# Another written order for the steps of a retention and GELU feed-forward kernel

## The chip, the cores and the metric

The kernel runs on one core of one Trainium2 chip. The metric is device time in microseconds (us): the median of three runs of the kernel before is 294.59 (294.44 to 296.1).

## What is computed

Two stages follow one another: retention (linear attention with a decay by distance) over 8 batches, 8 heads, 576 positions and 64 values per head, and a feed-forward layer with a tanh-GELU over the 4608 resulting rows.

```
q, k, v: (8, 8, 576, 64)     w_in: (512, 2048)     w_out: (2048, 512)

scores = q @ k.T / 8
gamma  = 1 - 2 ** (-5 - head)
ret    = scores * where(i >= j, gamma ** (i - j), 0)      # i: row of q, j: row of k
attn   = ret @ v
x      = attn with the heads side by side                 # (8 * 576, 512)
h      = x @ w_in
g      = 0.5 * h * (1 + tanh(sqrt(2 / pi) * (h + 0.044715 * h ** 3)))
out    = g @ w_out                                        # (4608, 512)
```

## The kernel before

**Units.** Each batch of 576 rows is cut into five units: four of 128 rows and a tail of 64, so unit u is part u % 5 of batch u // 5, and there are 40. The products of decay powers with q and v stand for the decay matrix; between the parts of a batch a state (sum of k times v) is carried in f32 and cast to f16 for the products. Units 0, 2, 5 and 7 are "wide": each of them stands for two units that are handled together (0 and 1, 2 and 3, and so on). The feed-forward layer goes in nine blocks t of 512 rows and sixteen groups fc of 128 hidden columns. From block 5 on the first product, and for most row pairs the second one, is a Strassen-Winograd product: seven block products instead of eight, with sums of blocks before (SBUF, VectorE) and after (out of PSUM).

**The order is written out by hand.** The string ORDER (line 17) is a list of 1369 steps; a loop at the end of the kernel calls one small function for each. The five engines and their queues run asynchronously, but each one takes its own instructions in the order in which the steps stand, so the string sets what stands behind what on TensorE (PE), VectorE (DVE), ScalarE (ACT), GpSimd (POOL) and SyncE (SP, which issues the loads, stores and DMA transposes). The steps that the change and the prediction speak of:

- `L,u,n` loads page n of unit u (0 is q, 1 is k, 2 is v) from SP (lines 206 to 241). A page is a slot of a pool of 21, nine once the feed-forward sums need the room; a load takes the slot that has been free longest, and its program waits for the cast that last read it. The program also lets every SP copy wait for the one eight before it.
- `I,g` and `J,g` load an eighth of w_in and of w_out, with a cast to f16, from GpSimd's queue (line 255). I,6 and I,7 serve columns 1536 to 2047 (fc 12 to 15), I,2 and I,3 fc 4 to 7, I,0 and I,1 fc 0 to 3, I,4 and I,5 fc 8 to 11; each pair is two halves of the sum over 512.
- `b`, `c`, `g` make the decay tables, the masks with the row powers gend, and the row powers gseg; `Z,i` zeroes a buffer of the f16 state; `w` loads ScalarE's table of the GELU.
- `q,u`, `k,u`, `v,u` scale or cast a page to f16 (lines 441 and 457, line 286 for a plain cast), `t` transposes it on PE (line 514) and `y` copies that out; `D,u` is the DMA transpose of later units (line 504). A last letter says by which engine: v VectorE (the default of q), g GpSimd, a ScalarE.
- `X` (line 640) and `Y` (line 657) are state products and scores of a wide unit, `m` the product with the mask out of PSUM (lines 665 and 722), `R` the attention product of a wide unit (lines 686 and 698), `B,u,w` the scores of unit u and the attention product of unit w, `a`, `o` and `z` the state's sum, decay and cast (lines 746, 754, 764 and 286), and `x` the copy of the result to xT in f16 (lines 607 to 620). There is one PSUM buffer for scores, two banks of pool h and two of pool o.
- `N,t,fc,half` is the first feed-forward product for two fc and half of the 512 rows, `M,t,fc` for one fc and all rows, `M,t,fc,part` for four fc and a quarter of the rows (all at line 790); `F` and `G` are their GELU out of PSUM (line 798).
- `O,t,u` is a quarter of a plain second product (line 816). `H`, `T` are sums for the second Winograd product, `W` (line 904) its block products, `V` its sums and copies out; `U`, `s` are sums for the first one, `A` (line 1001) its products, `l` its sums and copies and `f` its GELU (line 1019). `S` is a store. The sums are at line 850, where all Winograd sums have one helper: they are told apart by tile, tsum and ssum (T, H), pages and hc (U, s, l), ost (V).
- `K,n` is n products of the identity with itself, whose result nobody reads (line 1046).

The loop that calls them:

```
    for step_ in steps:
        name, *args = step_.split(",")
        do[name](*[int(a) if a.lstrip("-").isdigit() else a for a in args])
```

Of the kernel before, what the change touches and what calls it, by code (L numbers as in the profile page):

```python
# [24 lines left out]
N,0,0,1 G,0,9 J,2,g M,0,8 L,7,2 t,5,k,o z,3,1,v F,0,0,1 N,0,12,1 q,7,g G,0,8 y,5,k,a J,3,g N,0,14,1  # L25
Y,5,0 J,4,g k,7,g X,5 F,0,12,1 F,0,14,1 M,0,10 m,5,0 N,0,2,1 a,5,1,g J,7,g t,7,q,o L,9,0 a,6,1
G,0,10 B,-1,4 z,5,1,v Y,5,1 J,5,g m,5,1 M,0,11 F,0,2,1 N,0,6,1 t,7,k,o x,4 J,6,g y,7,k,v y,7,q,a R,5
O,0,4 O,0,0 o,6,1 F,0,6,1 Y,7,0 x,5 x,6 G,0,11 N,1,4,0 N,1,0,0 F,1,4,0 F,1,0,0 O,0,1 O,0,5 L,14,1
L,9,1 N,1,14,0 F,1,14,0 v,7,g H,0,1,5,v m,7,0 U,1,0 N,1,2,0 F,1,2,0 Y,7,1 X,7 L,9,2 a,7,1 z,7,1,a
N,1,10,0 O,0,6 N,1,6,0 F,1,6,0 m,7,1 q,9,g k,9,g a,8,1 z,6,1,v O,0,7 U,2,0 L,11,0 T,1,0,v e,0,1,v  # L30
H,0,1,2,v T,1,1,v R,7 v,9,g L,13,0 j,2,g F,1,10,0 D,9 T,2,1,v x,7 N,1,12,0 x,8 q,11 L,10,0 H,0,1,4,v
W,0,1,1 O,0,2 L,14,2 F,1,12,0 q,10,g L,10,1 N,1,12,1 L,11,1 F,1,12,1 T,2,0,v O,0,3 T,3,1,v B,9,-1
e,0,0,a T,4,0,v k,10,v V,0,1,0,v L,10,2 L,14,0 D,10 N,1,8,0 q,13 N,1,0,1 L,12,0 W,0,1,5 F,1,8,0
F,1,0,1 N,1,2,1 T,4,1,v N,1,14,1 F,1,2,1 L,11,2 k,11,g F,1,14,1 D,11 L,13,1 W,0,1,6 m,9 i,2,g
V,0,1,1,a N,1,8,1 T,3,0,v v,10,v j,4,g L,16,0 N,1,10,1 F,1,8,1 W,0,1,7 z,8,1,v B,10,9 V,0,1,3,a
L,12,1 x,9 m,10 V,0,1,4 N,1,4,1 W,0,1,4 F,1,10,1 a,10,0,g N,1,6,1 a,10,1 z,10,1,a W,0,1,3 v,11,g
z,10,0,v H,1,0,5,v B,11,10 V,0,1,5,v L,12,2 q,12 m,11 F,1,6,1 W,0,1,2 q,14 k,13,g a,11,0 F,1,4,1
W,1,0,1 x,10 N,2,10,0 L,15,0 V,1,0,0,a k,12,g N,2,14,0 H,1,0,2,v F,2,10,0 F,2,14,0 H,1,1,5,v V,0,1,6
V,0,1,2 v,12,v W,1,0,6 H,1,1,2,v L,16,1 j,3,v D,12 N,2,8,0 L,15,2 N,2,4,0 V,1,0,1,v L,13,2 D,13
L,15,1 a,11,1 o,11,1 z,11,0,a W,1,1,1 F,2,8,0 W,1,0,7 F,2,4,0 v,14,g B,12,11 V,1,1,0,v H,1,0,4,v  # L40
v,15,v i,5,a S,0,1 q,15,g a,12,0 z,11,1,a v,13,g i,0,a L,19,1 N,2,0,0 U,1,1 m,12 W,1,1,6 x,11 L,18,0
V,1,0,3,a z,12,0,g N,2,6,0 a,12,1 S,0,3 F,2,0,0 N,2,2,0 W,1,0,4 B,13,12 V,1,1,1,v k,15,v W,1,1,7
F,2,6,0 a,13,0 m,13 V,1,1,3,v V,1,0,5,a q,16 k,16,a W,1,0,2 a,13,1 N,2,12,0 k,14,g F,2,2,0 x,12
z,12,1,a N,2,14,1 D,14 F,2,12,0 W,1,0,5 z,13,1,v z,13,0,a W,1,1,4 S,0,0 L,16,2 B,14,13 L,18,2 L,17,1
F,2,14,1 V,1,1,5,a D,15 x,13 N,2,4,1 V,1,0,2,a L,17,0 L,17,2 H,1,1,4,v W,1,1,5 V,1,0,4,v F,2,4,1
N,2,12,1 L,24,0 v,16,g W,1,0,3 V,1,1,4,v F,2,12,1 m,14 N,2,0,1 B,15,14 V,1,0,6,v a,15,0,g k,17,v
S,0,2 m,15 F,2,0,1 N,2,10,1 W,1,1,3 F,2,10,1 H,2,0,5,v D,16 q,17 L,18,1 k,19,a N,2,2,1 L,20,0
# [1071 lines left out]
```

## Time and profile before

| | us |
|---|---|
| median of 3 runs (lowest, highest) | 294.59 (294.44, 296.1) |
| the profiled execution's own time | 295.5 |
| its span | 293.8 |
| TensorE busy | 280.0 |
| VectorE busy | 225.7 |
| ScalarE busy | 166.6 |
| GpSimd busy | 95.7 |

The span is the stretch that the profiler shows; the time of that execution is 1.7 us longer. Matmul rows carry a modelled end, so that neighbours overlap by some tens of ns. A row of a timeline gives start, duration, engine, line, operation, what it writes and reads, how many instructions were merged, and in brackets the idle time before it with what ended it. An engine's wait for several things is put down to the one that came last. Durations of GpSimd are rough. DMA-issuing rows of SP and GpSimd tell how long the issue took, not the transfer.

### The profile page before, as it was taken

What the parts mean: (1) busy time and instruction counts of PE and PEld (TensorE: products, weight loads), DVE (VectorE), ACT (ScalarE), POOL (GpSimd) and SP (SyncE); (2) the same over time, 40 slices, a digit from 0 to 9 for tenths busy, and PEclk for the clock granted to TensorE, in tenths of its full rate; (3) what the DMA queues carried; (4) which work ended last, traced back from release to release, by engine and by line L of the source; (5) the groups of instructions that cost most, each with busy time, mean ns of one, the idle gap of its engine ahead of it and who ended that gap; (6) DMA issues with size and microseconds to landing.
All of it is one profiled execution on the core that took longest, in us unless ns stands there. A gap on an engine that the chain in (4) does not pass through costs nothing.

```text
span 293.8 us, 9639 instructions
## 1 busy us (share of the span) xinstructions
PE 280.0 (95%) x4042; PEld 233.0 (79%) x4042; DVE 225.7 (77%) x446; ACT 166.6 (57%) x325; POOL 95.7 (33%) x157
## 2 busy tenths in 40 slices
PE   7697999999999999999999899999999999999995
PEld 2366767788888888888888778878887788888874
DVE  6684874986976798748758798899988989985841
ACT  2464763456655534656457558578576697655510
POOL 7841791202531321434643534644313301000000
PEclk9999999999999999999999999999999999999999
DMA  6999999949989979999998979997948430110112
GB/s 159 312 247 212 310 203 207 186 94 225 169 207 233 198 168 196 222 206 159 248 206 196 184 163 197 197 188 193 181 87 187 109 126 2 38 74 36 74 71 108
DMA packets 136428, 49.77 MB, mean 169 GB/s; under 512 B 118209, under 2 KB 130881, under 8 KB 136385
## 3 DMA queue, kind: packets, MB, share of 16 engines
q1 hardware_dynamic: 132032, 44.97, 70.6%
q0 software_dynamic: 4352, 4.20, 8.5%
q8 instruction: 31, 0.51, 0.8%
q14 instruction: 13, 0.10, 0.1%
HBM read 36.70 MB, written 9.44 MB: 157 GB/s over the span
## 4 chain that ended last, share of the span: by engine, by line
PE 77%; DVE 11%; DMA 5%; issue 2%; ACT 1%; SPq 1%; POOL 1%; DVEq 0%; POOLq 0%; ACTq 0%
PE bank L904 29%; PE bank L790 21%; PE bank L1001 14%; PE bank L816 4%; DMA w_in_sb<-in_moe_w_in_dram 3%; DVE ssum L850 2%; DVE pages L850 2%; PE sk L574 2%; PE x L550 2%; DMA pages<-in_q_dram 2%; PE sk L584 1%; PE x L595 1%; PE bank L1031 1%; DVE sz L764 1%; DVE hc L850 1%
## 5 line engine op out<-in xcount | busy, mean ns | idle before, releaser
L790 PE MATMUL bank<-xT,w_in_sb 128*128 128x256 f16 (+1 forms) x608 | 79.0, 279 | 1.8 <-ACT xT L607 0.9
L798 ACT ACTIVATE gT<-bank 128x512 f16<-128x512 f32 x80 | 47.0, 597 | 39.5 <-PE bank L790 39.2
L790 PEld LDWEIGHTS <-w_in_sb 128*128 128x128 f16 x608 | 57.5, 98 | 13.2 <-DMA w_in_sb<-in_moe_w_in_dram 2.5
L904 PEld LDWEIGHTS <-ssum 128*128 128x128 f16 x512 | 49.8, 98 | 6.8 <-DVE ssum L850 0.9
L904 PE MATMUL bank<-tsum,ssum 128*128 128x256 f16 x384 | 49.3, 273 | 0.3 <-DVE ssum L850 0.3
L904 PEld LDWEIGHTS <-gT 128*128 128x128 f16 x384 | 37.0, 98 | 4.4
L441 POOL TENSOR_TENSOR v<-pages,dec 128x512 f16<-128x512 f32 (+1 forms) x24 | 24.2, 1010 | 48.5 <-DMA pages<-in_v_dram 26.6
L286 POOL CAST sz<-s 64x256 f16<-64x256 f32 x36 | 17.3, 479 | 62.1 <-DVE s L746 51.6
L904 PE MATMUL bank<-w_out_sb,gT 128*128 128x256 f16 x256 | 32.9, 273 | 0.0
L1001 PEld LDWEIGHTS <-pages 128*128 128x128 f16 x256 | 24.2, 98 | 7.1 <-issue 2.9
L1001 PE MATMUL bank<-pages 128*128 128x256 f16 x192 | 27.9, 273 | 1.9 <-DVE pages L850 1.3
L722 DVE TENSOR_TENSOR ret<-sk,mask 128x512 f16<-128x512 f32 (+1 forms) x32 | 19.8, 618 | 9.8 <-PE sk L584 5.2
L850 DVE TENSOR_TENSOR ost<-u,bank 128x256 f32<-128x256 f32 x48 | 19.4, 416 | 9.5 <-PE bank L904 9.3
L850 DVE TENSOR_TENSOR ssum<-gT,ssum 128x1024 f16<-128x1024 f16 x32 | 24.0, 754 | 0.1
L284 ACT COPY hc<-bank 128x512 f32<-128x512 f32 x27 | 15.8, 586 | 14.1 <-PE bank L1001 13.8
L850 DVE TENSOR_TENSOR ssum<-gT 128x2048 f16<-128x2048 f16 (+1 forms) x20 | 21.3, 1063 | 2.7 <-ACT gT L798 2.1
L850 DVE TENSOR_TENSOR hc<-hc,bank 128x512 f32<-128x512 f32 x29 | 19.8, 684 | 4.0 <-PE bank L1001 3.8
L1001 PEld LDWEIGHTS <-w_in_sb 128*128 128x128 f16 x192 | 18.6, 98 | 2.9 <-DVE pages L850 0.6
L441 POOL TENSOR_TENSOR qk<-pages,dec 128x512 f16<-128x512 f32 (+1 forms) x16 | 17.1, 1070 | 9.7 <-DMA pages<-in_q_dram 4.8
L746 DVE TENSOR_TENSOR s<-s,sk 128x256 f32<-128x256 f32 x36 | 15.0, 416 | 5.8 <-PE sk L584 4.5
L1001 PE MATMUL bank<-xT,w_in_sb 128*128 128x256 f16 x128 | 19.2, 273 | 0.0
L1019 ACT ACTIVATE gT<-hc 128x512 f16<-128x512 f32 x29 | 17.8, 630 | 2.0 <-DVE hc L850 2.0
(117 smaller groups left out, 445.9 us busy)
## 6 DMA issues: line engine op xcount, KB each, us to landing
out_dram<-ost SPq DMA_DIRECT2D x35, 256.0 KB, 2.6
pages<-in_q_dram SPq DMA_DIRECT2D x32, 256.0 KB, 5.1
pages<-in_k_dram SPq DMA_DIRECT2D x24, 256.0 KB, 4.4
pages<-in_v_dram SPq DMA_DIRECT2D x24, 256.0 KB, 4.4
pages<-in_v_dram SPq DMA_DIRECT2D x4, 512.0 KB, 12.5
pages<-in_k_dram SPq DMA_DIRECT2D x4, 512.0 KB, 6.9
w_in_sb<-in_moe_w_in_dram POOLq DMA_DIRECT2D x8, 256.0 KB, 10.2
w_out_sb<-in_moe_w_out_dram POOLq DMA_DIRECT2D x8, 256.0 KB, 7.9
```

What stands on the lines that cost most here:

```text
L284: nc.scalar.copy(out=o, in_=i)
L286: (nc.vector if eng == "v" else nc.gpsimd).tensor_copy(out=o, in_=i)
L441: eng.tensor_tensor(out=out, in0=pages[:, page_of[s["u"], i], 0:n], in1=dec[:, i // 2, s["j"], 0:n].unsqueeze(2).to_broadcast([128, n, D]) ...
L722: nc.vector.tensor_tensor(out=ret[:, :, 0:n], in0=now["two"][:, :, 0, 0:n], in1=mask.unsqueeze(1).unsqueeze(1).to_broadcast([128, 2, n, G] ...
L746: nc.vector.tensor_tensor(out=s32, in0=state[0], in1=kv, op=ALU.add)
L790: nc.tensor.matmul(hps[:, i, :], w_in_sb[:, ct, 128 * (fc + i) : 128 * (fc + i) + 128], xT[:, ct, TB * t % XR + lo : TB * t % XR + hi], st ...
L798: nc.scalar.activation(out=gTs[t][:, fc : fc + TB // (hi - lo), lo:hi], in_=h.pop((t, fc, lo)), func=AF.Gelu_apprx_tanh, bias=0.0, scale=1.0,)
L816: nc.tensor.matmul(ops[t, tcc], gTs[t][:, ft, 128 * tcc : 128 * tcc + 128], w_out_sb[:, ft, :], start=(ft == 0), stop=(ft == NFC - 1),)
L850: (nc.vector if eng == "v" else nc.gpsimd).tensor_tensor(out=out, in0=a, in1=b, op=op)
L904: nc.tensor.matmul(p["ps", bank][:, HN * col : HN * col + HN], a[:, k], b[:, k], start=(k == 0 and fresh), stop=(k == HK - 1), skip_group_ ...
L1001: nc.tensor.matmul(p["ps", bank][:, n], w[:, c, 128 * n : 128 * n + 128], x[:, c], start=(n == 0 and c == 0 and i in (1, 2, 5)), stop=(c = ...
L1019: nc.scalar.activation(out=gTs[t][:, f : f + 2, o : o + 256], in_=p["ps", 0] if i == 0 else p["c", i], func=AF.Gelu_apprx_tanh, bias=0.0, ...
```

## The change

Only ORDER changes, from 1369 to 1371 steps. The steps up to the 279th and those behind the 540th stand in another order; in between (with a few swaps by one place) the two orders are the same. What is computed stays the same.

- Ahead of all stand now `b c g,g`, the tables and masks, and the first load is q of unit 0 (`L,0,0`), whose cast (`q,0,g`) follows at once; before, three other loads, a zeroing and the issue of one piece of w_in stood ahead of it. The load of k of unit 0 (`L,0,1`) moves from third to seventh among the L steps. v of units 0 and 2 is scaled by GpSimd instead of VectorE, q of unit 4 the other way round.
- In block 0 the four steps `M,0,8` to `M,0,11` and the halves `N,0,4` and `N,0,6` become four quarters `M,0,4,0` to `M,0,4,3` and halves `N,0,8` and `N,0,10`. `w` moves behind the first GELUs, so that ScalarE's table load stands ahead of the first of them.
- The first products of block 0 stand behind `Y,2,1`, `t,5,q`, `X,2` and `Y,2,0`; before, they stood ahead of them or among them. There are 35 dummy products for 38.
- Behind the 540th step loads, casts, sums and copies are in a new order and in part on other engines (of the V copies nine go from ScalarE to VectorE and eight the other way; of the state's casts ten leave GpSimd and seven go to it, and so on), and three pairs of ssum differences are split or joined (`H,6,0,5`, `H,7,0,5`, and `H,7,1,1` with `H,7,1,3`).

```diff
 ORDER = """
-Z,0,g L,4,1 L,0,2 L,0,1 Z,1,v g,g Z,3,v c k,0,a L,0,0 b I,6,g L,2,0 v,0,v K,4 K,4 K,4 K,4 t,0,k,h
-y,0,k,v q,0,g Z,5,v X,0 I,7,g K,4 K,1 t,0,q,h I,2,g L,2,1 q,2 y,0,q,v a,0,1,g z,0,1,a I,3,g a,1,1
-K,4,o K,3,o Y,0,1 L,2,2 Z,2,g L,4,0 m,0,1 k,2,a K,4 K,2 Y,0,0 m,0,0 o,1,1 t,2,k,h L,5,0 t,2,q,h
-y,2,k,a R,0 L,5,1 I,1,g y,2,q,v x,1 x,0 L,4,2 I,0,g z,1,1,g K,4 Y,2,0 L,5,2 L,7,0 k,4,v v,2,v
-t,4,k,o N,0,12,0 I,4,g N,0,14,0 w y,4,k,a X,2 m,2,0 a,2,1 F,0,12,0 F,0,14,0 L,7,1 a,3,1 Y,2,1 I,5,g
-z,2,1,g m,2,1 N,0,6,0 N,0,4,0 F,0,4,0 q,4,g F,0,6,0 R,2 x,3 t,4,q,o x,2 N,0,0,0 N,0,2,0 q,5 y,4,q,a
-v,4,g B,4,-1 F,0,0,0 m,4 Z,4,g J,1,g N,0,4,1 F,0,2,0 t,5,q,o M,0,9 y,5,q,v k,5,v v,5,v J,0,g F,0,4,1
...
+b c g,g L,0,0 L,4,1 L,2,0 L,0,2 L,4,0 q,0,g K,4 K,4 K,4 K,4 K,1 t,0,q,o y,0,q,v L,2,2 q,2 I,2,g K,4
+K,4 K,4 K,1 t,2,q,o L,0,1 y,2,q,v Z,3,v k,0,a t,0,k,o v,0,g y,0,k,a q,4 Z,2,g K,4 K,1 Y,0,0 k,4,a
+Z,5,v X,0 t,4,q,h I,3,g L,2,1 L,5,0 Z,1,v k,2,a a,0,1,g m,0,0 K,4,o Y,0,1 t,2,k,o Z,0,g a,1,1 I,7,g
+I,6,g z,0,1,a v,2,g t,4,k,o m,0,1 I,0,g o,1,1 L,5,1 R,0 y,2,k,a q,5 Y,2,1 I,1,g L,4,2 x,1 m,2,1
+t,5,q,o x,0 X,2 L,5,2 I,4,g z,1,1,a Y,2,0 I,5,g Z,4,g M,0,4,0 y,4,k,a a,2,1 v,4,g z,2,1,v y,4,q,v
+M,0,4,1 a,3,1 J,1,g m,2,0 G,0,4,0 k,5,v N,0,14,0 R,2 G,0,4,1 J,0,g z,3,1,v B,4,-1 J,2,g y,5,q,v
+N,0,12,0 F,0,14,0 x,2 t,5,k,o N,0,0,0 F,0,12,0 y,5,k,v x,3 m,4 L,7,0 J,3,g F,0,0,0 N,0,2,0 F,0,2,0
...
-m,22 F,4,12,0 V,3,1,1,v F,4,12,1 z,22,0,g M,4,0 B,23,22 G,4,0 L,26,2 V,3,0,3,v W,3,0,4 a,23,0 L,27,1
-m,23 q,25 z,22,1,v k,24,g V,3,0,5,a z,23,0,v M,4,2 x,22 N,4,6,1 W,3,1,7 v,25,g a,23,1 q,27,g G,4,2
-v,26,g V,3,1,3,a N,4,6,0 v,24,g k,27,a W,3,0,5 k,26,v z,23,1,g D,24 F,4,6,1 F,4,6,0 B,24,23 L,30,1
...
+W,3,1,6 m,22 F,4,12,0 F,4,12,1 z,22,0,g V,3,1,1,v M,4,0 B,23,22 G,4,0 L,26,2 V,3,0,3,v W,3,0,4
+k,24,g L,30,0 q,25 a,23,0 L,27,1 q,27,g m,23 z,22,1,v V,3,0,5,a z,23,0,v M,4,1 k,27,g x,22 v,24,g
+N,4,6,0 W,3,0,5 k,26,a a,23,1 z,23,1,v F,4,6,0 W,3,0,2 W,3,1,7 V,3,1,3,v G,4,1 D,24 L,29,0 v,25,g
...
+z,33,1,g k,38,v V,5,0,5,a L,35,2 W,5,1,4 B,34,33 V,5,1,5,v q,35,g A,6,2,7 H,5,0,4,v
+W,5,0,5 v,35,g k,35,a A,6,2,5 l,6,2,2,a l,6,2,4,v x,33 L,37,0 q,37 A,6,2,4 L,39,2 W,5,0,2 m,34
+V,5,0,4,v A,6,2,3 D,35 f,6,2,0 D,36 f,6,2,2 L,37,1 A,6,3,1 f,6,1,3 L,38,0 B,35,34 l,6,2,5,v
...
```

More of the change, by code (lines that the diff above doesn't have):

```diff
@@ L28 @@
[L28 to L39, printed above, removed]
@@ new lines @@
+i,7,a l,8,3,1,v S,6,3 W,7,0,2 l,8,3,3,v f,8,2,3 f,8,2,2 A,8,3,7 j,7,g S,7,1 V,7,0,2,a l,8,3,2,v
+W,7,1,3 A,8,3,5 V,7,0,6,v i,3,a f,8,3,1 A,8,3,4 V,7,1,6,v W,8,0,1 l,8,3,4,v W,7,1,2 A,8,3,3 S,7,3
+f,8,3,0 S,7,0 V,8,0,0,a H,8,0,1,v H,8,0,2,v W,8,0,6 V,7,1,2,a W,8,0,5 V,8,0,1,v f,8,3,2 W,8,0,2
+l,8,3,5,v W,8,0,7 H,8,0,4,v f,8,3,3 V,8,0,3,v P,2 W,8,0,4 V,8,0,2,a V,8,0,4,v V,8,0,5,v W,8,0,3
+S,8,1 O,8,8 O,8,9 S,7,2 O,8,10 O,8,11 E,2,a V,8,0,6,v e,8,2,v S,8,0 P,0 E,0,v S,8,2 Q,2 Q,0 P,1
+E,1,a j,0,a i,1,a Q,1
```

153 lines of the change are left out of this document (79 added, 74 removed).

## The prediction, made before the change was run

> **What bounds the kernel now.** I read the busy shares first, then the stretches of 10 us, then the queues of GpSimd and SyncE over the first 24 us, then the waits. The page:
>
> ```profile
> span 293.8 us, 9639 instructions
> PE 280.0 (95%) x4042; PEld 233.0 (79%) x4042; DVE 225.7 (77%) x446; ACT 166.6 (57%) x325; POOL 95.7 (33%) x157
> ...
> DMA  6999999949989979999998979997948430110112
> ```
>
> TensorE (PE) is idle for 293.8 - 280.0 = 13.8 us, and 10.9 us of its busy time are the dummy products of the K steps (38 at line 1046, of 0.22 to 0.24 us back to back). An order that keeps the real work can win nothing but parts of these. The stretches say where they lie:
>
> ```profile
> 0.00:10.00 10.00, 5.85 (x24) 2.35 (x24) 5.73 (x49) 2.70 (x4) 7.22 (x41) 1.00 0.73 215
> 10.00:20.00 10.00, 9.65 (x170) 5.42 (x167) 8.96 (x11) 4.90 (x8) 7.82 (x11) 1.00 1.18 267
> 20.00:30.00 10.00, 8.22 (x151) 6.49 (x151) 5.05 (x7) 5.84 (x12) 1.66 (x4) 1.00 1.20 220
> ...
> 160.00:170.00 10.00, 9.23 (x132) 7.91 (x130) 8.49 (x17) 5.59 (x12) 5.08 (x7) 1.00 0.83 168
> ...
> 190.00:200.00 10.00, 9.35 (x134) 8.05 (x132) 9.57 (x19) 7.42 (x15) 4.81 (x8) 1.00 0.88 185
> ...
> 220.00:230.00 10.00, 8.98 (x124) 7.64 (x117) 8.46 (x15) 6.86 (x13) 5.02 (x6) 1.00 0.74 158
> ```
>
> Columns: stretch, its length, busy us of PE, weight loads, VectorE, ScalarE, GpSimd, then TensorE's granted clock (1.00 throughout), DMA share, GB/s. The idle time is 4.15 + 0.35 + 1.78 + 0.47 = 6.75 us up to 40 us, 0.26 up to 160, 3.7 from 160 to 280 (0.77, 0.37, 0.65, 0.07, 1.02, 0.29, 0.29, 0.24), and some 3.1 behind the last product at 290.7. The changed steps are the first 279 (products up to about 75 us) and those behind the 540th (from about 140 us). So two stretches matter: the head, and 160 to 280 us.
>
> In the head, the timelines of GpSimd and of PE:
>
> ```profile
> 8.25 0.90 POOL L255 DMA_DIRECT2D w_in_sb<-in_moe_w_in_dram  x1
> 9.97 1.90 POOL L457 TENSOR_TENSOR wide<-pages,decw 128x1024 f16<-128x1024 f32 x1 [0.82 <-DMA pages<-in_q_dram]
> 11.82 2.20 POOL L255 DMA_DIRECT2D w_in_sb<-in_moe_w_in_dram  x3
> ```
> ```profile
> 19.64 2.21 PE L790 MATMUL bank<-xT,w_in_sb 128*128 128x256 f16 x16
> ...
> 23.49 1.70 PE L790 MATMUL bank<-xT,w_in_sb 128*128 128x256 f16 x14 [0.71 <-DMA w_in_sb<-in_moe_w_in_dram]
> ...
> 27.37 1.92 PE L790 MATMUL bank<-xT,w_in_sb 128*128 128x256 f16 x16 [0.94 <-ACT xT L607]
> ```
>
> The reader is to see that the first scaled q is ready only at 11.87, and that, once the first feed-forward products run (19.64), the weights hold them: the fourth piece of w_in is issued at 13.2 and lands at 23.45. I put 27.37 down to the sixth piece too, issued at about 15.2 and 10.9 to 12.2 us under way: ScalarE's copy of xT, which is named, is of columns that these products don't read. The 40 slices have the DMA engines at 0.9 or more from the second slice on, so a piece that is issued later lands later. My measure is the time that PE has not spent on real work: by 27.37 it was busy for 5.85 + 9.65 + 5.6 = 21.1, less 10.9 of dummies, so 10.2 real and **17.1 us lost**.
>
> **The change part by part.** Real products are the same: the four full-width M steps of feed-forward columns 1024 to 1535 become halves, and columns 512 to 1023 become quarters: 64 products of 128 columns, at the 0.055 us of back-to-back transposes (8 in 0.44), are 3.5 us, 16 of 512 are 16 x 0.22 = 3.5. Nothing. Dummies: 35 for 38, -0.7 us at most, hidden, since what follows waits for data. All k, q, v, z, l and V that change engine: VectorE gains nine V copies and loses eight (+0.4), and by the same counts l -0.7, z +0.8, v -3.5 (two of 1.22 in the head), q +1.1, k -0.4, y +1.6, a +0.4; one more pair of ssum differences is taken in two halves (+0.1). That is -0.2 of 225.7: nothing.
>
> *q first.* SP's first two copies are now q of unit 0 (0.65 each, so out by 2.15); with nothing ahead I take 5 to 6 us for landing (before: issue 3.5 to 4.8, landed 9.80). GpSimd has its tables done at 4.06 + 0.75 + 1.42 + 1.45 = 7.7 (mask, gend, gseg; a zeroing of 0.58 and an issue of 0.90 go behind). The cast runs 7.7 to 9.6, 2.2 earlier than now. That alone buys nothing: *k of unit 0* falls from the fourth SP copy to the eleventh, behind k of unit 4, q of 2, v of 0, q of 4 and v of 2. (Each SP copy waits for the eighth before it, so the last three stand behind q's landing too.) Its end is then the 2.8 MB mark of SP's queue. Before, k of unit 2 was at 2.6 MB and landed at 13.0. Ends: 11.3 (the better start, 2 KB runs first) to 13.4; I take 12.5, nearest that row. Then cast 1.04, transposes 0.6, copy 1.01, latencies: scores of unit 0 (Y,0,0) at 15.3, where the earlier of Y,0,1 and Y,0,0 was at 14.13. The mask product (1.23) frees the scores' one bank at 17.0, the 4 dummies end at 17.4, Y,0,1 0.4, mask 1.23: the first attention product ends at 19.7 (now 18.27). Behind it on VectorE stand old 0.41, q of unit 5 1.22 and the mask of Y,2,1 1.22: 21.95, and **PE's queue has Y,2,0, which waits for that bank, ahead of the first feed-forward product**: 22.45 instead of 19.64. Not 2.8 us lost, since t,5, X,2 and both Y,2 are done by then, which stood behind it.
>
> *Weights.* GpSimd's issues become: I,2 at 9.65; v of unit 0 (1.90; it moved here from VectorE) 10.4 to 12.3; zeroing 0.56; I,3 at 12.9; zeroing; I,7 and I,6 at 14.1 and 14.9; v of unit 2 (1.90); I,0, I,1, I,4, I,5 at 17.5 to 19.7. At today's 9.6 to 10.9 us of landing: second piece 22.5, fourth 25.7, sixth 28.6. First product at 22.45 fits; N,0,14,0, after two quarters of 0.88, is at 24.2 and would wait for the fourth piece, 0 to 1.5 us. Then R,2, B,4, N,0,12,0, t,5,k: 2.9; so N,0,0,0 starts between 28.0 and 29.4. By then 1.3 more real work is done than before the same step today (both t,5 and B,4): 11.5, so 16.5 to 17.9 lost against 17.1. **Head: +0.3, ends -1.8 (k at 11.3, no wait for weights) and +3.5 (below).** Moving ScalarE's gelu table load (1.28) behind the unit's xT copies lies in the same wait (first gelu about 23.3). SP's other loads are in nearly the same sequence up to v of unit 5, so the bytes ahead are those of today.
>
> *Behind step 540.* The 3.7 us of idle PE follow VectorE, at 8.5 to 9.6 of 10 there, in sums it makes for PE: waits on `pages` (xsum, hc) are 1.6 us, hc 0.8. Among these sums are some that take two to three times their usual time while GpSimd works:
>
> ```profile
> L764 DVE TENSOR_TENSOR sz<-s,gend x12: 405/422/3177, 33.8 to 247.8; 64x256 f16<-64x256 f32 x12
> ```
> ```profile
> L850 DVE TENSOR_TENSOR ssum<-gT,ssum x32: 676/684/1520, 55.3 to 280.3; 128x1024 f16<-128x1024 f16 x32
> ```
>
> (two views by line and by tile; least, median, longest ns). The change moves sums against GpSimd's steps. Laying both orders along PE's work, and each GpSimd step from where it stands for its row's time, VectorE's SBUF sums and casts behind step 540 overlap GpSimd for about 18 us of their 52 before and 20 of 51 after: no sign of a gain. New risks: k of unit 27 goes into the page that k of unit 24 has only just left, and waits on GpSimd ahead of four v; q of unit 37 is cast right behind its load. A load lands a median of 4.4 (k) or 5.1 us (q) behind its issue, so each could hold its engine for that long; against it, GpSimd waits for sums for 62 us in all, so it can run ahead, and q's page is free long before. I take **0, ends -3 and +3**.
> [...]
>
> Sum: 295.5 (the profiled execution; span 293.8 and 1.7 around it) + 0.3 + 0 = 295.8; the median of the runs is 0.9 lower, so **294.9**.
>
> **Rivals.** *Faster:* sums stand clear of GpSimd, and most of the 3.7 us goes; the head gives 0.5 (k early). -3.5: 291.0. For: long rows such as 1.78 for two sz casts at 189.6 (0.58 usual), just before PE's 0.65 us. Against: the overlap above, and that waits move to the next sum. 0.20. *Slower:* GpSimd's two v casts ahead of six of the eight w_in pieces. Place: POOL's queue, line 457. If v of unit 0 lands after 10.4, or that of unit 2 after 15.6 (it landed at 16.2 today, with 3.1 MB ahead of it; 2.3 now), every later piece slips by as much, and PE stops at N,0,14,0 and again at N,0,0,0. v at 12.5 and 17.5: I,3 at 15, I,0 at 19.5, N,0,0,0 at 31.5 less 11.5: 20 lost, +3. It decides once I,1 is issued behind 18.5. With a loss of 0.5 in the tail: 298.4. 0.32. *It does not do what it says:* q's cast still starts near 10, because its tables or SP's first copy are late; then the k chain hides it anyway: 294.9, within the forecast's 0.48.
>
> **How the numbers follow.** One per cent, 2.9 us, is about what a measurement of this kernel can tell from no change. Forecast 0.48 (its own range 291.6 to 297.5); the slower rival mostly lies beyond 297.5 and the faster below 291.6: faster 0.20, same 0.48, slower 0.32. The range leaves out the outer third of each rival: 291.3 to 299.3.
>
> **What would show it.** Right: GpSimd's first line-457 product starts at 7.7 to 8; ScalarE's cast of k at 11.3 to 13.4; first line-790 product at 21.5 to 23.5; then waits for w_in of at most 1.5 us; PE busy about 280 less 0.7, idle 160 to 280 us of 2 to 5 us. Wrong: w_in waits of over 3 us in sum before 32 us; a PE wait over 1 us on L574 or L584 around units 27, 35 or 37; or idle below 1.5 us behind 160.

## The result, and the profile after

The changed kernel takes 296.91 us (median of 18 runs, 295.09 to 299.88) against 294.83 (18 runs of the kernel before beside them, 293.63 to 296.83): a ratio of 1.0065, 95% interval 1.0042 to 1.0087. Ratios here leave out executions that lie over 1.5% above the fastest of their kernel, so that they can be below the quotient of the medians. The forecast was 294.9 with a range of 291.3 to 299.3. The profiled execution took 297.25 us, span 295.3; before, 295.5 and 293.8. ORDER is one line longer now, so a line is one higher: L791 is the L790 of before, L1002 the L1001, L851 the L850.

The page of the changed kernel:

```profile
span 295.3 us, 9743 instructions
...
PE 280.9 (95%) x4091; PEld 235.7 (80%) x4091; DVE 220.3 (75%) x449; ACT 168.3 (57%) x330; POOL 95.0 (32%) x150
```

TensorE is busy for 0.9 us longer, 0.7 of it in dummy products (11.6 against 10.9: there are 39 for 38, in runs of 17, 13, 5 and 4, not the 35 that I had counted), and VectorE for 5.4 us less, in nearly as many instructions as before (449, 446). Fewer VectorE microseconds for the same sums is the first sign that something got out of its way.

The stretches of 10 us of the changed kernel (stretch, length, busy us of PE, weight loads, VectorE, ScalarE, GpSimd, clock, DMA share, GB/s):

```profile
0.00:10.00 10.00, 6.44 (x19) 2.31 (x20) 4.07 (x46) 1.75 (x3) 7.97 (x40) 1.00 0.72 205
10.00:20.00 10.00, 8.21 (x121) 4.61 (x120) 7.68 (x10) 4.38 (x7) 7.35 (x8) 1.00 1.13 272
...
40.00:50.00 10.00, 9.24 (x158) 6.97 (x151) 6.45 (x10) 4.29 (x9) 0.34 (x1) 1.00 1.08 197
...
160.00:170.00 10.00, 9.49 (x136) 8.35 (x134) 7.71 (x19) 6.57 (x15) 1.93 (x4) 1.00 1.04 233
...
190.00:200.00 10.00, 10.00 (x188) 8.93 (x186) 8.78 (x19) 7.76 (x16) 2.73 (x5) 1.00 0.85 165
...
220.00:230.00 10.00, 9.97 (x137) 8.63 (x135) 8.66 (x21) 6.95 (x13) 2.36 (x4) 1.00 0.59 165
```

Two things stand here. The second stretch has 8.21 where it had 9.65, and 40 to 50 us has an idle 0.76 that it didn't have: the head got worse. And the three stretches that were at 9.23, 9.35 and 8.98 stand at 9.49, 10.00 and 9.97: from 160 to 280 us PE is idle for 1.7 us instead of 3.7.

To see where the two kernels part I use the products of k and v that open step B of each unit (line 574, now 575), which follow one another in the same sequence in both. The first of them starts at 71.12 us (before 68.18), so 2.94 late; the twelfth is 2.95 late (147.64), the thirteenth 2.08 (155.99), the 19th 1.18 (198.33), the 23rd 0.38 (234.17). Behind the 540th step these marks are rough, since other products have moved around them (the 21st is 4.20 late). PE's last product ends at 291.11, before at 290.69: 0.42 late. The span is 1.5 longer all the same: **the head costs 2.9, the steps behind the 540th win 2.5, and 1.1 is lost behind the last product.**

The head, GpSimd's timeline in the changed kernel:

```profile
7.92 1.90 POOL L458 TENSOR_TENSOR wide<-pages,decw 128x1024 f16<-128x1024 f32 x1
...
11.00 1.89 POOL L458 TENSOR_TENSOR wide<-pages,decw 128x1024 f16<-128x1024 f32 x1 [0.33 <-DMA pages<-in_v_dram]
...
18.29 1.89 POOL L458 TENSOR_TENSOR wide<-pages,decw 128x1024 f16<-128x1024 f32 x1 [2.32 <-ACT qk L285]
20.14 2.91 POOL L256 DMA_DIRECT2D w_in_sb<-in_moe_w_in_dram  x4
```

q of unit 0 is scaled at 7.92, 2.05 us earlier than before. Then SP's queue, ScalarE and PE:

```profile
7.43 2.39 SPq L221 DMA_DIRECT2D pages<-in_k_dram  x1
9.86 1.37 SPq L221 DMA_DIRECT2D pages<-in_k_dram  x1
```
```profile
14.59 1.04 ACT L285 CAST wide<-pages 128x1024 f16<-128x1024 f32 x1 [8.46 <-DMA pages<-in_k_dram]
```
```profile
17.41 0.42 PE L658 MATMUL sk<-qkT 64*64 64x128 f16 x16
...
24.34 1.07 PE L791 MATMUL bank<-xT,w_in_sb 128*128 128x128 f16 x16
...
30.41 1.92 PE L791 MATMUL bank<-xT,w_in_sb 128*128 128x256 f16 x16 [0.33 <-ACT gT L799]
```

The early q waits for k: ScalarE sits idle for 8.46 us and has k of unit 0 at 14.59. The issue of that copy, the first of the two rows, took 2.39 us, where one takes 0.6 in the same queue; it landed 7.1 us after its issue began. Before, too, the eleventh copy of SP's queue was held at its issue (3.07 us from 8.04 on). Scores come at 17.41, the first feed-forward product at 24.34 (before 19.64), and no product waits for w_in any more. N,0,0,0 starts at 30.41, 3.04 later than before, with 1.2 us more of real work done by then (22.95 us busy less 11.6 of dummies, against 21.1 less 10.9): 1.9 lost. The other 1.0 up to 68 us: 0.3 more of idle time (k of unit 7, of which below), and 0.7 that stands as busy time of PE and that I can't lay to a row.

The two groups that I had shown as stretched, and the sums of xT, in the changed kernel by line (least, median, longest ns):

```profile
L765 DVE TENSOR_TENSOR sz<-s,gend x14: 405/419/423, 27.7 to 247.9; 64x256 f16<-64x256 f32 x14
```
```profile
L851 DVE TENSOR_TENSOR ssum<-gT,ssum x32: 677/684/1198, 59.1 to 280.7; 128x1024 f16<-128x1024 f16 x32
...
L851 DVE TENSOR_TENSOR pages<-xT x8: 418/419/426, 167.3 to 251.2; 128x512 f16<-128x512 f16 x8
L851 DVE TENSOR_TENSOR pages<-xT,pages x8: 418/419/975, 169.3 to 254.0; 128x512 f16<-128x512 f16 x8
```

The longest sz product was 3177 and is 423. The sums of xT (`pages<-xT`) have a mean of 421 and 488 ns; before, 591 and 612 (busy us, mean ns of one, idle before):

```profile
L850 DVE TENSOR_TENSOR pages<-xT,pages 128x512 f16<-128x512 f16 x8 | 4.9, 612 | 0.2
L850 DVE TENSOR_TENSOR pages<-xT 128x512 f16<-128x512 f16 x8 | 4.6, 591 | 0.8 <-ACT xT L614 0.8
```

Why, is seen in the four timelines around 167 us. Before, VectorE and GpSimd:

```profile
167.34 1.26 DVE L850 TENSOR_TENSOR pages<-xT 128x512 f16<-128x512 f16 x1
...
169.78 1.26 DVE L850 TENSOR_TENSOR pages<-xT,pages 128x512 f16<-128x512 f16 x1
```
```profile
167.13 1.19 POOL L441 TENSOR_TENSOR v<-pages,dec 128x512 f16<-128x512 f32 x1 [2.08 <-DMA pages<-in_v_dram]
168.27 1.04 POOL L286 CAST sz<-s 64x256 f16<-64x256 f32 x2
169.40 1.36 POOL L441 TENSOR_TENSOR qk<-pages,dec 128x512 f16<-128x512 f32 x1
```

And the changed kernel:

```profile
167.35 0.76 DVE L851 TENSOR_TENSOR pages<-xT 128x512 f16<-128x512 f16 x2
...
169.28 0.42 DVE L851 TENSOR_TENSOR pages<-xT,pages 128x512 f16<-128x512 f16 x1
```

Before, each sum of 0.42 us lay beside a GpSimd product and took 1.26; in the changed kernel GpSimd is idle from 166.1 to 170.0 us, and two sums fit in 0.76. PE's wait of 0.77 at 168.66 behind the first is gone. From 150 to 290 us PE waited for VectorE's `pages` and `hc` for 2.4 us before (total, times, longest us), and for 0.4 in the changed kernel:

```profile
PE bank L1001 <- DVE pages L850: 1.6, 3, 0.8
PE bank L1001 <- DVE hc L850: 0.8, 2, 0.7
```

The end, VectorE's timeline, before and then in the changed kernel:

```profile
288.09 0.69 DVE L286 COPY ost<-bank 128x512 f32<-128x512 f32 x1 [3.03 <-PE bank L816]
```
```profile
289.75 1.07 DVE L287 COPY ost<-bank 128x512 f32<-128x512 f32 x2 [4.26 <-DMA out_dram<-ost]
```

Before, the last wide copy waits for PE; now for a store that must leave one of the four ost buffers. The stores of 256 KB from 284 us on took a median of 4.5 us to land (before 2.2). Behind PE's last product there are 4.2 us instead of 3.1.

### The profile page after: what moved, and what is told of

Its sections match the earlier page's. It is cut to its first block, busy times and chain, and to the rows that moved or that the text cites. A ratio compares the mean times of both kernels' runs of the same rounds, so it can differ in the third digit from the quotient of the medians.

```text
span 295.3 us, 9743 instructions
## 1 busy us (share of the span) xinstructions
PE 280.9 (95%) x4091; PEld 235.7 (80%) x4091; DVE 220.3 (75%) x449; ACT 168.3 (57%) x330; POOL 95.0 (32%) x150
## 4 chain that ended last, share of the span: by engine, by line
PE 81%; DMA 8%; DVE 4%; SPq 2%; ACT 1%; issue 1%; ACTq 0%
PE bank L905 32%; PE bank L791 19%; PE bank L1002 17%; DMA pages<-in_k_dram 8%; PE bank L817 4%; PE sk L575 2%; PE x L551 2%; PE sk L585 1%; PE x L596 1%; PE bank L1032 1%; SPq L239 1%; SPq L216 1%; PE bank L1047 1%; DVE ssum L851 1%; PE sk L658 1%
## 5 line engine op out<-in xcount | busy, mean ns | idle before, releaser
L791 PE MATMUL bank<-xT,w_in_sb 128*128 128x256 f16 (+1 forms) x656 | 79.2, 270 | 0.6 <-ACT gT L799 0.3
L791 PEld LDWEIGHTS <-w_in_sb 128*128 128x128 f16 x656 | 59.8, 98 | 10.5 <-issue 0.9
L442 POOL TENSOR_TENSOR v<-pages,dec 128x512 f16<-128x512 f32 (+1 forms) x26 | 28.3, 1097 | 51.2 <-DMA pages<-in_v_dram 26.8
L287 POOL CAST sz<-s 64x256 f16<-64x256 f32 x34 | 15.6, 460 | 43.5 <-DVE s L747 33.4
L1002 PE MATMUL bank<-pages 128*128 128x256 f16 x192 | 27.9, 273 | 0.5 <-ACT hc L285 0.3
L1002 PEld LDWEIGHTS <-pages 128*128 128x128 f16 x256 | 24.5, 98 | 4.4 <-issue 1.4
L851 DVE TENSOR_TENSOR ost<-u,bank 128x256 f32<-128x256 f32 x48 | 19.4, 415 | 9.2 <-PE bank L905 9.2
L851 DVE TENSOR_TENSOR ssum<-gT 128x2048 f16<-128x2048 f16 (+1 forms) x21 | 21.1, 1005 | 4.2 <-ACT gT L799 3.8
L851 DVE TENSOR_TENSOR hc<-hc,bank 128x512 f32<-128x512 f32 x29 | 19.9, 685 | 4.4 <-PE bank L1002 3.2
L851 DVE TENSOR_TENSOR ssum<-gT,ssum 128x1024 f16<-128x1024 f16 x32 | 22.7, 710 | 0.1
L1002 PEld LDWEIGHTS <-w_in_sb 128*128 128x128 f16 x192 | 18.5, 98 | 2.9 <-issue 0.7
L1002 PE MATMUL bank<-xT,w_in_sb 128*128 128x256 f16 x128 | 19.2, 273 | 0.0
L615 ACT ACTIVATE xT<-x 128x512 f16<-128x512 f32 (+1 forms) x25 | 14.4, 580 | 6.5 <-PE x L596 6.3
```

What stands on the lines that cost most here:

```text
L287: (nc.vector if eng == "v" else nc.gpsimd).tensor_copy(out=o, in_=i)
L442: eng.tensor_tensor(out=out, in0=pages[:, page_of[s["u"], i], 0:n], in1=dec[:, i // 2, s["j"], 0:n].unsqueeze(2).to_broadcast([128, n, D]) ...
L615: nc.scalar.activation(out=xT[:, :, o : o + G * (b - a)].rearrange("c p (h s) -> c p h s", s=G), in_=x[:, a:b].rearrange("c h p s -> c p h ...
L791: nc.tensor.matmul(hps[:, i, :], w_in_sb[:, ct, 128 * (fc + i) : 128 * (fc + i) + 128], xT[:, ct, TB * t % XR + lo : TB * t % XR + hi], st ...
L851: (nc.vector if eng == "v" else nc.gpsimd).tensor_tensor(out=out, in0=a, in1=b, op=op)
L1002: nc.tensor.matmul(p["ps", bank][:, n], w[:, c, 128 * n : 128 * n + 128], x[:, c], start=(n == 0 and c == 0 and i in (1, 2, 5)), stop=(c = ...
```

## The experiments

The marks below are the lateness against the profile of before, at the first of the products of line 574 (68 us) and at PE's last product. All ratios are to the kernel before, run on the same chip.

**e1: the head alone.**

```diff
+ORDER = the change's first 280 steps, then before's from its 280th on
```

> The first 279 steps as in the changed kernel, everything behind them as before. Theory (head and tail are separate effects): the changed head puts the products at 68 us back by 2.9 us, and nothing behind it takes that up, since TensorE is over 99% busy from there to 150 us: 297.7 against 294.8 (ratio 1.010). Rival (the idle TensorE time behind 160 us is slack in front of data that come at a fixed time, so a later start is partly absorbed there): at most 1 us slower, ratio 1.000 to 1.003.

1.0105 (1.0065 to 1.0144), median 299.21; +4.00 at 68 us, +4.34 at the last product. The head's timeline is the changed kernel's (first product 24.18, N,0,0,0 at 30.16), but the wait for k of unit 7 is 1.92 us instead of 0.47 there. So the head is a loss by itself, of 3 to 4 us with that wait, as the theory had it, and it also brings the late store at the end.

**e2: the steps behind the 540th alone.**

```diff
+ORDER = before's first 279 steps, then the change's from its 281st on
```

> The first 279 steps as before, everything behind them as in the changed kernel. Theory: the new tail wins 2.5 us of TensorE time by itself (xsum sums no longer stretched beside GpSimd): 292.3, ratio 0.991 to 0.993. Rival 1 (the new tail only looks good because it starts 2.9 us later, with loads and casts further ahead): 294.8, ratio 0.998 to 1.002. Rival 2 (the 1.1 us that the last stores cost in the profile of the changed kernel belong to the new tail): 293.4, ratio 0.995.

0.9972 (0.9945 to 0.9998), median 294.95 against 295.77: the best of all kernels here. +0.20 at 68 us, -1.63 at the last product: 1.8 won. It has no late store (2.2 us). Its sums of xT have means of 428 and 421 ns. The ratio is less of a gain than the theory's 0.991 to 0.993, and its interval reaches into the first rival's 0.998 to 1.002, so a later start may have a part in the 2.5 us of the changed kernel. The two halves together, 1.0105 times 0.9972, make 1.0077, about the change's 1.0065.

**e3: k of unit 0 directly behind q.**

```diff
-L,0,0 L,4,1 L,2,0 L,0,2 L,4,0 ... L,2,2 ... L,0,1
+L,0,0 L,0,1 L,4,1 L,2,0 L,0,2 L,4,0 ... L,2,2
```

> The changed kernel with one step moved: the load of k of unit 0 stands directly behind that of q of unit 0. Theory (the late k, cast at 14.6, is what holds the head): k is cast by 8, the transposes of q of unit 2 (14.0) then end the wait, scores of unit 0 at about 15.6 instead of 17.4, first feed-forward product at 22.5 instead of 24.3; 1.8 us less than the changed kernel, ratio to before 1.001. Rival (v of unit 0 and the weights, which now land later, or the one score bank hold it anyway): first feed-forward product still behind 23.8, ratio to before 1.005 to 1.008.

1.0065 (1.003 to 1.01), median 298.54: nothing won on the changed kernel. k is cast at 7.49, scores are at 15.29, 2.1 earlier, the first feed-forward product at 23.36. But then, on GpSimd and on PE:

```profile
11.71 2.93 POOL L458 TENSOR_TENSOR wide<-pages,decw 128x1024 f16<-128x1024 f32 x1 [1.06 <-DMA pages<-in_v_dram]
...
15.06 0.76 POOL L256 DMA_DIRECT2D w_in_sb<-in_moe_w_in_dram  x1
```
```profile
28.43 1.89 PE L791 MATMUL bank<-xT,w_in_sb 128*128 128x256 f16 x8 [2.64 <-DMA w_in_sb<-in_moe_w_in_dram]
```

The cast of v of unit 0 holds GpSimd till 14.6, the second piece of w_in goes out at 15.06, and PE stops for 2.64 us. In this profile its clock then is 0.50 for some 3.4 us (means of 0.92, 0.50 and 0.73 over the three stretches of 2 us from 26 us on). So late k is not the only thing that can be in the way: behind it stands the weights' queue. But the profiled execution was the longest of the eleven (295.1 to 300.85 us): it shows what can happen, not what the median execution lost.

**e4 and e5: engines alone, order alone.** Behind step 551 the change alters both where a step stands and, for 60 steps, on which engine it runs.

```diff
 e4: before's order; 60 steps behind the 551st with the change's engine
-k,27,a ... q,29,g ... z,30,0,g ... V,6,0,0,a
+k,27,g ... q,29   ... z,30,0,v ... V,6,0,0,v
 e5: the change's order there; the same steps with before's engine
```

> The kernel before with only the engine letters behind step 551 as in the changed kernel (60 steps change engine, none its place). Theory (the tail's gain comes from where the xsum sums stand against GpSimd's steps): q of unit 29 leaves GpSimd, which takes away one of the stretched sums ahead of block 5; others stay; 0 to 1 us faster, ratio 0.997 to 1.000. Rival (the gain is that VectorE's load is spread otherwise): all 2.5 us come from the letters, ratio 0.992.

> Before's first 551 steps; behind them the change's order, but each step on the engine it has before (the complement of the run with the engines alone). Theory: the order is what clears VectorE's sums of GpSimd's steps, and the engine letters alone were a loss only because they stood in an order not made for them: 0 to -1.6 us to before (293.0 to 294.6 on the scale of before's 294.6), the sums of xT for the h products again near 0.42 us, PE idle 160 to 280 us of 1.5 to 3 us. Rival: order and letters only fit together, and the order with the old engines costs as the letters alone did, +3 us or more (297.6 and up).

e4: 1.0195 (1.0165 to 1.0225); -0.28 at 68 us, +5.84 at the last product. e5: 1.0188 (1.0155 to 1.0221); +0.78 at 68 (PE was idle for 2.67 us in the head and its clock at 0.50 from 10 to 16 us), +6.50 at the last product, so 5.7 lost behind the head. PE's waits from 150 to 290 us (total, times, longest us) in e4:

```profile
PE bank L1001 <- DVE pages L850: 2.3, 3, 1.3
PE bank L904 <- DVE ost L850: 1.5, 3, 0.6
PE bank L1001 <- DVE hc L850: 1.1, 2, 0.7
```

For e5 the first is `ost` with 1.6, and before had 1.6 on `pages`, 0.8 on `hc`. Each half costs some 6 us, both together win 2. Neither expectation of e4 came. In e5 one half of the theory held, as its sums of xT show:

```profile
L851 DVE TENSOR_TENSOR pages<-xT,pages 128x512 f16<-128x512 f16 x8 | 3.3, 417 | 0.0
L851 DVE TENSOR_TENSOR pages<-xT 128x512 f16<-128x512 f16 x8 | 3.3, 420 | 0.6 <-ACT xT L621 0.5
```

The order by itself clears these sums, but PE is idle for 5.65 us from 160 to 280 us all the same, on other waits, and the time is the rival's. So clear sums alone don't win; order and engines fit only each other.

**e6 and e7: the instruction fetch.** e1 and e3 have the late store, e2 and e4 don't; what the first two share is the changed head with 49 products and 49 weight loads more on PE. The page counts the instruction packets (queue, packets, MB, share). Before and after:

```profile
q8 instruction: 31, 0.51, 0.8%
```
```profile
q8 instruction: 32, 0.52, 0.8%
```

One packet is 16 KB (0.52 MB in 32). The last one falls between 276 and 278 us before, between 284 and 286 after, where the last stores go out.

```diff
 e6: before, the first 16 dummy products / e7: the changed kernel, the first 24
-nc.tensor.matmul(t, ident, <512 columns of ident>)
+for j in range(4): nc.tensor.matmul(t[:, j], ident, ident)
```

> Before with 16 of its 38 dummy products of 512 columns each made as four of 128 columns: the same TensorE time, 48 products and 48 weight loads more, 96 instructions, about as many as the change adds (98). Theory (instruction fetch): PE's program now needs one block more; the page's count of instruction packets goes from 31 to 32, one of them stands at 281 to 287 us of the span, beside the last stores, which then take 4.4 to 4.7 us to land instead of 2.2 to 2.4, and the kernel ends 1.1 us later while its products end where they did: ratio to before 1.0037. Rival (the late store comes from something else in the changed head, the loads' order or where its tiles lie): 31 packets or stores of 2.2 to 2.4 us, ratio 1.000.

> The changed kernel with 24 of its 35 dummy products made as four of 128 columns each: 144 instructions more on PE, the same TensorE time. Theory (instruction fetch): PE takes some 28 instructions per us, so the last block is fetched some 5 us earlier, near 279 us, clear of the last stores; these land in 2.2 to 2.4 us, and more instructions make the changed kernel about 1.1 us faster: ratio to before 1.003 instead of 1.0065. Rival (something else in the head): stores of 4.4 us again, ratio 1.0065.

e6: 32 packets, the last at 286 to 288 us, stores of 3.1 us, and VectorE's last wide copy waits 3.59 for a store. So 96 instructions bring the late store into a kernel that had none. But the end is not later (3.0 us behind the last product): here the stores that the copy waits for land early enough. 1.0013 (0.9984 to 1.0043) doesn't tell 1.0037 from 1.000. e7: the last packet is at 280 to 282, stores take 2.5 us, and the last wide copy waits for PE again:

```profile
290.37 0.69 DVE L287 COPY ost<-bank 128x512 f32<-128x512 f32 x1 [3.03 <-PE bank L817]
```

3.0 us behind the last product instead of 4.2. 1.0045 (1.0017 to 1.0074) lies between the two expectations, and the median of all twelve runs is 297.91, 1.008 of before's: the times show no gain. In the trace the theory stands. It does in the other kept traces too: in all seven whose last fetch starts 1.0 to 2.1 us behind the issue of the first of these stores (the changed kernel, e1, e3, e6, e8, e10, e12) the stores take 3.1 to 4.6 us and VectorE's last wide copy waits for one; in the seven where it is 5 us or more ahead of that issue they take 2.0 to 2.5 and the copy waits for PE. Behind the last product stand 3.0 to 4.3 us in the first seven (3.8 in the mean) and 3.0 to 3.6 in the others (3.2), so the price is nearer 0.6 us than the 1.1 of this one pair of profiles. In e7's profile another thing cost 1.4 at 68 us: k of unit 0 was 2.1 us later than in the changed kernel. PE's timeline, and two stretches of 2 us (the clock is the third number from the right):

```profile
17.75 1.04 PE L515 MATMUL bank<-ident,wide 128*128 128x128 f16 x8 [3.27 <-ACT wide L285]
```
```profile
16.00:18.00 2.00, 0.25 (x3) 0.25 (x4) 0.84 (x4) 1.04 (x1) 0.00 (x0) 0.86 1.15 288
18.00:20.00 2.00, 2.00 (x12) 1.17 (x10) 0.00 (x0) 1.18 (x2) 0.00 (x0) 0.50 1.17 262
```

**e8: k early, and v of units 0 and 2 on VectorE.**

```diff
 e3, and
-v,0,g ... v,2,g
+v,0,v ... v,2,v
```

> Before behind step 551 is not in this one: it is the changed kernel with k of unit 0 loaded directly behind q, as in the run before, and with the casts of v of units 0 and 2 on VectorE instead of GpSimd. Theory (the head is a chain through k on the one side and GpSimd's queue of weights on the other, and both must be freed): pieces of w_in are issued at 9.8, 10.7, 12.2 and by 16.5; first product of L791 at 23 to 24, waits for w_in under 1 us in sum, N,0,0,0 at 28 to 29, so PE 2 to 3 us earlier at 68 us than in the changed kernel; ratio to before 0.995 to 1.000. Rival (VectorE is the bound of the head once it takes 2.4 us of casts: its masks and the q casts come later by as much): first product at 25 or later, no gain on the changed kernel, 1.005 or more.

1.0151 (1.0105 to 1.0197), slower than the changed kernel: the rival was right (first product at 25.80). No product waits for w_in, but masks and casts on VectorE are late (PE waits 0.70, 0.43, 1.24 and 1.11 us for them from 16 to 24 us); PE was busy for 3.3 us of the six from 16 to 22, and from 24 to 30 its clock is 0.50. +5.25 at 68 us.

**e9: GpSimd put beside the sums.** e2, with a useless sum of xT on GpSimd just ahead of each of VectorE's 16 sums for the h products; its result goes into the mask of the wide units, which is no longer read.

```diff
     def sum_x(t, i, eng="v"):
+        nc.gpsimd.tensor_tensor(out=beside, in0=x, in1=b[1][0], op=ALU.add)
         combine(eng, s[i - 1], x, y, ALU.add if i in (2, 3) else ALU.subtract)
```

> The kernel with before's head and the change's order behind it (0.9972 of before), and 16 useless sums on GpSimd: each of VectorE's 16 sums of xT for the h products (stages 5 to 8) gets a GpSimd sum of the same 512 columns, with the same operand from xT, put just ahead of it, so that both become ready together. Theory (VectorE's sums with both operands in SBUF are held while GpSimd reads SBUF, and TensorE waits for just these sums): their mean goes from 0.42 to 0.49 us back to 0.6 to 1.2 us, PE waits for them at L1002, and idle PE from 160 to 280 us goes from about 1.5 to 3 us or more: 1.5 to 4 us slower than that kernel, ratio to before 1.002 to 1.011. Rival (what I counted on: such stretching is lost among other waits and doesn't reach the end): sums may stretch, but the ratio stays at 0.997, within 0.002.

1.032 (1.0275 to 1.0365). VectorE's groups (busy us, mean ns of one, idle before), and PE's waits from 150 us on:

```profile
L851 DVE TENSOR_TENSOR pages<-xT 128x512 f16<-128x512 f16 x8 | 7.1, 902 | 1.9 <-ACT xT L621 1.3 <-PE bank L1004 0.5
L851 DVE TENSOR_TENSOR pages<-xT,pages 128x512 f16<-128x512 f16 x8 | 5.9, 740 | 0.0
```
```profile
PE bank L1004 <- DVE pages L851: 3.6, 3, 2.4
PE x L551 <- POOL sz L287: 3.2, 1, 3.2
PE bank L1004 <- DVE hc L851: 1.4, 2, 1.0
```

The sums went from 428 and 421 ns to 902 and 740, and PE waits for what they feed, 5.0 us where e2 had no such wait of size: the mechanism is there, and it reaches the end. 1.032 is more than the theory's 1.002 to 1.011, but the whole of the 11.8 us that the last product is later than in e2 isn't the price of the mechanism: the added sums stand in GpSimd's queue and hold the state's casts behind them (3.2), and behind two of the waits the clock is at 0.50 for some 3.4 us each (means of 0.60 and 0.55 over the two stretches of 2 us from 170 us on, of 0.63 and 0.51 from 204), which is some 3.4 us of work at full clock, an estimate from these means.

**e10 and e12: k early and five pieces of w_in ahead of the v casts.**

```diff
 e3, and
-v,0,g ... I,3,g ... I,7,g I,6,g ... v,2,g ... I,0,g ... I,1,g
+I,3,g I,7,g I,6,g v,0,g ... I,0,g I,1,g v,2,g
```

> The changed kernel with k of unit 0 loaded directly behind q, and with five pieces of w_in issued ahead of GpSimd's two v casts: I,3, I,7 and I,6 ahead of v of unit 0, I,0 and I,1 ahead of v of unit 2. Theory (with k early the head is held by the pieces that stand behind those casts, and nothing else): pieces at 9.8 to 12.9 and 15 to 16.5 us; scores of unit 0 at 15.3; first product of L791 at 23 to 23.5; waits for w_in under 0.5 us in sum where the run with k alone has 2.9; N,0,0,0 at 28 to 29; PE's granted clock 1.00 throughout; PE at most 1.5 us behind before at 68 us; ratio to before 0.995 to 1.001. Rival (the pieces that go out earlier take the DMA engines from k, v and q): scores of unit 0 after 16.5 or the first product after 24.3, and no gain on the changed kernel: 1.005 or more.

In e10's profile, on GpSimd and PE:

```profile
9.75 3.04 POOL L256 DMA_DIRECT2D w_in_sb<-in_moe_w_in_dram  x4
12.81 1.92 POOL L458 TENSOR_TENSOR wide<-pages,decw 128x1024 f16<-128x1024 f32 x1
```
```profile
23.40 2.91 PE L791 MATMUL bank<-xT,w_in_sb 128*128 128x128 f16 x40
```

Scores at 15.29, first product at 23.40, no wait for w_in, N,0,0,0 at 28.95, clock 1.00: the head that was expected. By N,0,0,0 only 0.6 us is lost against before, where the changed kernel has 1.9: late k and the pieces behind the casts are most of that. It is +2.16 at 68 us where I had put 1.5 at most (0.93 of it k of unit 7), and -0.24 at the last product. That execution took 296.3 us. But the twelve runs lie between 295.6 and 305.8, median 300.0, ratio 1.0085 (1.0053 to 1.0117), by the medians 1.015: the time didn't follow. e12 is the same kernel, for a second profile:

> The kernel with k early and the pieces first once more, for a second profile: its times lay between 295.6 and 305.8 us, and the profiled execution was one of the shortest (296.3). Theory (the spread is TensorE's clock: in the longer executions a load is late, PE is idle for more than about 2.5 us in the head, and the clock is at 0.50 for some us behind it): a profile of 299 us or more has a granted clock under 1.00 in the first 50 us, behind such an idle time, and its feed-forward products start as much later. Rival (the loads alone): the clock is 1.00 throughout, and the time is lost in waits for DMA in the head or behind it. A profile near 296 tells neither.

299.1 us, clock 1.00 up to the last product, so this execution is the rival's. The head is as in e10 (+1.72 at 68), and the loss stands at 156 us, on GpSimd and PE:

```profile
153.11 0.61 POOL L287 CAST qk<-pages 128x512 f16<-128x512 f32 x1 [3.85 <-DMA pages<-in_k_dram]
153.69 4.06 POOL L442 TENSOR_TENSOR v<-pages,dec 128x256 f16<-128x256 f32 x4
```
```profile
158.54 0.32 PE L585 MATMUL sk<-qkT 64*64 64x64 f16 x16 [2.22 <-DMA qkT<-qk]
```

That is k of unit 27 in GpSimd's queue ahead of four v products, 2 us later than in e10; the scores wait 2.22 for a DMA transpose. It explains this execution. Those of 302 to 306 us have no profile, but the mean granted clock of each execution is on record, and it goes with the theory: 1.00 in the two shortest of e10 (295.6 and 296.3), 0.994 or less in the ten others, 0.983, 0.981 and 0.978 in the three longest, and 0.983 in e12's other execution of 303.02. A mean of 0.978 over a span of 303.9 us is 6.7 us of work at full clock, an estimate from these two numbers. So much of the spread goes with the clock; what brought it down there stays open.

**e11: dummies in the gap ahead of k.**

```diff
 e7, and
-t,0,k,o
+K,4 K,2 t,0,k,o
```

> The changed kernel with the 24 split dummies of the run before, and six more dummy products just ahead of the transposes of k of unit 0, 1.3 us of TensorE's time in the gap where it waits for that k. In the profiled run with the split dummies k came late, PE was idle for 3.27 us and its granted clock went to 0.50 for about 4 us behind. Theory (TensorE's clock is halved behind an idle time of over about 2.5 us, and in part of the runs of the changed kernel k is late enough for that): the gap falls under 2.5 us, the clock stays at 1.00, the runs spread less than 294.8 to 301.0, and the ratio to before is 1.000 to 1.003 instead of 1.0045. Rival (the spread comes from the loads themselves): same spread, ratio 1.0045 or, by the 1.3 us of dummies, more.

Median 296.27 (294.89 to 299.01), 1.0024 (0.9996 to 1.0052); clock 1.00, no idle time over 0.4 us between 10 and 20 us. The limit of about 2.5 us in the theory was my estimate from the profiles before: 2.45 us with 1.00 behind it (e1), 2.64 and 2.67 with 0.50 (e3, e5). It doesn't hold: in e9 the clock is at 0.50 behind 2.37 us, in e11's own profile at 1.00 behind 2.52 (up to 9.88). Against e7 (294.75 to 301.0) it goes the way the theory says, but the intervals overlap. The clocks on record say more: a mean of 0.994 or less in one of e11's twelve executions, in seven of e7's twelve, in eight of the changed kernel's 18, and in nine of 71 of before in the rounds of these experiments.

## Why the prediction came out near, and where it was wrong

The time lies in the range and the change is within the one per cent, but +0.3 us was forecast and a loss of 0.65% (some 2 us) measured, and the sum came that near by luck, by three errors that partly cancel: +0.3 + 0 + 0 forecast, +2.9 - 2.5 + 1.1 measured in the span.

- *q first buys nothing.* Right: cast at 7.92 (forecast 7.7), and it waits for k.
- *k of unit 0 at 12.5, at most 13.4.* **This is the step that failed in the head.** It came at 14.59. I laid its landing by the bytes ahead of it, from a row of a copy at nearly the same mark. But that copy was issued at 6.78 and landed 6.2 us later, at 13.0; this one went out from 7.43 on, was held at its issue (2.39 us) and landed 7.1 us later. Even at 6.2 it would have been 13.6. In e3 the copy is issued at 2.17 and cast at 7.49. From there every forecast mark is late by nearly as much: scores 17.41 for 15.3, first product 24.34 for 22.45 (window to 23.5), N,0,0,0 at 30.41 for 28.0 to 29.4. The "lost" time by my own measure is 30.41 - 22.95 + 11.6 = 19.1 where I had 16.5 to 17.9.
- *k of unit 7* I had not looked at. It costs 0.5 in the changed kernel and 1.9 in e1.
- *Weights: 0 to 1.5 us of waiting.* Measured none, for the wrong reason: the pieces went out even later than I had them (the last four from 20.14 on), but the products that need them came later still. The slower rival's mechanism, v casts ahead of the pieces, was real and covered by the late k: the profile of e3 uncovers it (2.9 us of waits), and by its own deciding point (I,1 issued behind 18.5) it would have been forecast for the changed kernel. That point left out that PE itself can be later.
- *Engine letters, -0.2 us: nothing.* The counts were right and the conclusion wrong. e4 shows those behind step 551 as 6 us of loss in another order. A step's price is what waits behind it where it stands.
- *Behind step 540: 0.* **This is the step that failed in the tail**, -2.5 (e2 alone: -1.8). I had counted the overlap of VectorE's sums with GpSimd's steps along the written order, 18 against 20 us, and read from it that nothing would change. The count treats all overlap alike, and lays GpSimd's steps from where they stand, while they run when loads and pages let them (in the changed kernel a load ended the 3.91 us of idle time before GpSimd's cast at 169.99). The rows tell another thing: it matters which sums are met, and those of xT around 167 us, for which PE waits, went from 1.26 to 0.42 us. The faster rival had this mechanism, at 0.20. e9, where a GpSimd sum stands beside each of these, has them at means of 902 and 740 ns for 428 and 421. The tail won 2.5, where that rival had about 3. How much of it the sums are is not isolated: PE's waits for `pages` and `hc` fell by 2.0 us, and e5 has clear sums and loses.
- *Risk of k of unit 27.* Named, and taken as covered. In the changed kernel's profile GpSimd waits 2.60 us for it and PE doesn't; in e12 PE does. So it can be one source of the wider spread.
- *It does not do what it says.* Fell: q's cast was early.
- *35 dummies, quarters of M: nothing.* There are 39 dummies, a miscount: not 0.7 us less but 0.7 more, in waits all the same. The time of the 64 quarters is as forecast (4.2 us, against 4.1 for the 16 products of 512 columns that they replace). But these 48 products more and the one more dummy are, with their weight loads, 98 more instructions on PE, and the page counts 32 instruction packets for 31, the last of them between 284 and 286 us, among the last stores: 1.1 us in this profile, in no term of my sum.

## What to carry to other kernels

Ask of a step that is moved ahead not when it can run but when its partner is there: an early q is worth nothing before its k, and once k is early the next queue can be the bound. An order and the engines of its steps are one choice, so don't price them apart. Where PE waits for sums in SBUF, look at what GpSimd does at that very moment, sum by sum (0.42 us where GpSimd was idle, 1.26 beside its product); the total of the overlap, 18 against 20 us, didn't show the gain.

## What the runs showed of the hardware

- Stores that ran beside a packet of the instruction queue landed later: the last 256 KB stores took a median of 4.5 to 4.6 us where the last packet (16 KB: 0.52 MB in 32) fell into them (1.1 us behind the start of their issue in the changed kernel, 2.0 in e1), 3.1 in e6 (1.9 behind), and 2.2 to 2.5 where it was clear of them (before, e2, e7). Through the buffers that the stores must free, this was 1.1 us at the end of the changed kernel and some 0.6 by the means over all profiles.
- PE's granted clock fell to 0.50 around idle times of 2.64 (e3), 2.67 (e5), 3.27 (e7), and 2.37 and 3.21 us (e9), and in e8 behind six us (16 to 22) in which PE was busy for 3.3; around 2.12 (before), 2.45 (e1) and 2.52 (e11) it stayed at 1.00. So the length of the idle time alone doesn't tell the two groups apart, and what else counts no run here shows. By the means over stretches of 2 us, taken as a mix of 1.00 and 0.50, it stayed at 0.50 for some 3.4 us each time in e3, e7 and e9 (in e7 0.86, 0.50 and 0.79 from 16 us on) and for some 6.8 in e5 and e8 (in e8 0.79, then three times 0.50, from 22). Eight products of 256 columns took 1.89 us in such a stretch and 1.05 behind it (e3, at 28.43 and 31.74). At 0.50, 3.4 and 6.8 us are 1.7 and 3.4 us of work at full clock, an estimate from these lengths, on top of the wait itself.
- Still open: 0.7 us of PE's busy time in the head, and what brought the clock down in the longer executions of e7, e10 and of the changed kernel.
